# Two sequences feed the early expert tiles, routing goes out in steps, and the next tile's rows are turned between the two products

## The chip, the core and the metric

One Trainium2 chip, one of its cores. Its engines run side by side, each through its own queue of instructions in order: TensorE (PE, with its weight loads PEld), VectorE (DVE), ScalarE (ACT), GpSimd (POOL), and SyncE (SP), which issues most transfers. The metric is the device time of one launch in microseconds, lower is better.

## The reference

Block-sparse attention, then a cosine router that sends each token to one of eight experts. Shapes: 4 sequences, 8 heads, 768 tokens, head size 64; 3072 tokens of width 512; expert products 512x1024 and 1024x512, all in fp32.

```python
# q, k, v: (4, 8, 768, 64); the mask lets a block of 32 see its neighbours,
# the first and last block, and 3 sampled blocks
scores = where(mask, (q @ k.T) / sqrt(64), -1e9)
attn = softmax(scores) @ v
x = attn.transpose(0, 2, 1, 3).reshape(3072, 512)
xn = x / (norm(x) + 1e-6);  en = expert_emb / (norm(expert_emb) + 1e-6)
logits = xn @ en.T / tau                      # (3072, 8)
e = argmax(logits, 1)
gate = 1 / (sum(exp(logits - max(logits))) + 1e-9)
out[i] = gate[i] * (relu(x[i] @ w1[e[i]]) @ w2[e[i]])
```

## The kernel before

**Attention** (`attention_fast`) works on 16 pairs of heads, four pairs to a sequence. A pair has 12 units of work: two halves of the queries by six chunks of 128 keys. In a unit `u` TensorE multiplies scores for unit `u + 2` (`score_fast`, tile `sc`; the mask goes in as a small bf16 product), ScalarE takes the exponential (tile `e`), and TensorE multiplies `e` with `v` (`attend_fast`, tile `av`), while VectorE adds up the exponentials (tile `esum`). Every sixth unit ends a half: ScalarE copies one half of `av` to the tile `part` (L321), VectorE adds the other (tile `at`, L323), and the pair to come is turned (`turn_fast`, tiles `kt` and `qt`). `av` has one buffer: the next half's first product waits for `at`. Three units later `settle` turns the result back to rows (tile `back`) and divides by the sum. It also squares the rows on GpSimd (tile `sq`, L365) and adds the squares on VectorE (tile `nsq`, L366), for the norm. The small turns of `turn_fast`, `settle`, `rank`, `count` and `fill_slots` share one two-bank PSUM buffer (`two_banks`).

**Routing.** At the fifth unit of the next sequence `route` is issued for the finished one in a single piece: the norm's square root on GpSimd (L416), logits, maximum, one-hot choice and gate on VectorE, one exponential on ScalarE (L440), then the rows with their gate are written to `x_dram` (and `x_early`). Ten units later `rank` numbers the tokens of each expert. Once `EARLY` = 3 sequences are routed, `dispatch_early` picks `NE` = 11 tiles of 128 tokens, each tile of one expert alone, in six pieces at six units of the last sequence: counts, experts (`expert_e`), places, lanes (tile `lanes`), slots (`slot_e`). Two units later `fetch` is issued for the tiles 0 and 1: two loads of 2 MB for `w1` and `w2`, and one gather of the 128 rows (tile `xg`).

**Expert tiles** (`expert_tiles`). In all 27 tiles run: 24 always (`NE + NU`), the others under nested conditions on the number used. Each iteration fetches tile `i + 2` and runs `expert_tile(i)`: four turns of the gathered rows (tile `xg_ps`), a copy on VectorE (tile `xgt`), the first product in 64 matmuls into `hp` (two PSUM banks, two buffers), ReLU of its first half on ScalarE (L661) and of its second on VectorE (L662, both into `h`), the second product in 16 matmuls (tile `yp`), the gate on VectorE (tile `y`), and an indirect write to the output. The last sequence's `settle` and `route` are issued ahead of the first tile; its `rank` and `dispatch_late`, which finds the other tiles, lie between the first tiles (`between`), and must be through before tile `NE` is fetched.

A planner orders each engine's instructions by priority (the order of the program) among those whose inputs it expects to be ready, and sets all waits. Work under a condition stays in its block.

## Time and profile before

| | |
|---|---|
| median of 3 runs | 829.29 us (828.89 to 829.34) |
| profiled execution, its own time | 829.78 us |
| span of its instructions | 828.1 us |
| mean granted TensorE clock | 0.977 |
| TensorE busy | 768.2 us, 93% of the span |
| VectorE busy | 332.3 us, 40% |
| ScalarE busy | 200.6 us, 24% |
| GpSimd busy | 103.2 us, 12% |
| DMA, mean | 202 GB/s |

Times in the profile are microseconds from the start of the span. A matmul that is busy is not one at its peak, since matmuls overlap; so the pace of a stage is read from the distance of two starts. In brackets behind an instruction stands how long its engine sat idle before it, and what ended that.

### The profile page before, as it was taken

To read this page: it belongs to the slowest core of one execution; us is meant where nothing else is said; L and a number is where in the kernel's file an instruction comes from. 1 tells how busy PE (TensorE), PEld (TensorE's weight loads), DVE (VectorE), ACT (ScalarE), POOL (GpSimd) and SP (SyncE) were. 2 spreads that over 40 slices of the span, in tenths; PEclk is the share of its full clock that TensorE was granted. 3 is DMA by queue.
4 is the path that set the end of the run, shared out by engine and by line. 5 is a ranking of instruction groups with operands and counts; after the bars stand their busy time and mean duration, and the time that the engine had idled before them with its cause. 6 is when DMAs were issued, how large, how long until landed. Compare 5 with 4: busy or idle time off the path is not lost.

```text
span 828.1 us, 22309 instructions
## 1 busy us (share of the span) xinstructions
PE 768.2 (93%) x10026; PEld 502.6 (61%) x10026; DVE 332.3 (40%) x669; ACT 200.6 (24%) x292; POOL 103.2 (12%) x138
## 2 busy tenths in 40 slices
PE   5999979999799979789899999999999999999883
PEld 2555545555455545555667667677676776776661
DVE  3666666667666666755562111111111111111000
ACT  2555544554455534334100000000000000000000
POOL 2000010000100010030212011011010110100110
PEclk9999989999999999999899999999999999999997
DMA  4111243121411143750799889989888899888880
GB/s 155 31 51 58 60 152 119 61 59 61 182 47 51 54 172 99 272 188 4 281 331 313 293 309 323 315 308 326 318 307 308 303 331 319 297 317 304 287 288 16
DMA packets 64242, 167.04 MB, mean 202 GB/s; under 512 B 3004, under 2 KB 15292, under 8 KB 63238
## 3 DMA queue, kind: packets, MB, share of 16 engines
q1 hardware_dynamic: 59382, 151.17, 52.9%
q0 software_dynamic: 4480, 13.91, 4.3%
q8 instruction: 82, 1.34, 0.6%
q10 hardware_dynamic: 272, 0.39, 0.1%
q14 instruction: 26, 0.21, 0.1%
HBM read 148.14 MB, written 18.11 MB: 201 GB/s over the span
## 4 chain that ended last, share of the span: by engine, by line
PE 80%; DVE 6%; issue 6%; ACT 3%; DMA 1%; POOL 1%; SPq 0%; POOLq 0%; ACTq 0%
PE hp L658 21%; PE yp L666 20%; PE sc L296 17%; PE av L317 15%; PE turn L279 2%; PE back L352 2%; ACT h L661 2%; DVE esum L314 2%; PE back L345 1%; ACT e L299 1%; DMA out_dram<-y,slot_l 1%; POOL nrm L416 1%; DMA emb<-in_moe_expert_emb_dram 1%; DVE nsq L366 0%; DVE x L360 0%
## 5 line engine op out<-in xcount | busy, mean ns | idle before, releaser
L658 PEld LDWEIGHTS hp<-xgt,w 128*128 128x128 f32 x1728 | 200.5, 193 | 30.2 <-ACT h L661 12.4
L658 PE MATMUL hp<-xgt,w 128*128 128x128 f32 x1728 | 206.7, 278 | 12.7 <-ACT h L661 6.9
L666 PE MATMUL yp<-w,h 128*128 128x512 f32 x432 | 189.9, 592 | 0.0
L299 ACT ACTIVATE e<-sc 128x768 f32<-128x768 f32 x192 | 155.5, 810 | 132.9 <-PE sc L296 132.8
L317 PE MATMUL av<-e,vld 64*64 64x384 f32 x1536 | 169.3, 504 | 15.7 <-DVE at L323 15.1
L296 PE MATMUL sc<-qt,kt 64*64 64x384 f32 x1536 | 165.2, 495 | 0.0
L314 DVE TENSOR_TENSOR esum<-esum,e 128x768 f32<-128x768 f32 x128 | 122.4, 956 | 71.8 <-ACT e L299 69.6
L666 PEld LDWEIGHTS yp<-w,h 128*128 128x128 f32 x432 | 80.0, 190 | 90.4 <-issue 90.2
L661 ACT ACTIVATE h<-hp 128x512 f32<-128x512 f32 x27 | 16.1, 597 | 381.0 <-PE hp L658 381.0
L317 PEld LDWEIGHTS av<-e,vld 64*64 64x64 f32 x1536 | 53.0, 135 | 67.6 <-issue 23.7
L296 PEld LDWEIGHTS sc<-qt,kt 64*64 64x64 f32 x1536 | 62.0, 137 | 40.7 <-issue 38.0
L668 DVE TENSOR_SCALAR y<-yp,xg 128x512 f32<-128x512 f32 x27 | 20.3, 751 | 158.4 <-PE yp L666 158.4
L296 PE MATMUL sc<-qmask,kmask 64*64 64x384 bf16 x768 | 69.8, 333 | 0.0
L365 POOL TENSOR_TENSOR sq<-x 128x384 f32<-128x384 f32 x32 | 26.5, 827 | 332.3 <-DVE part L367 237.2
L662 DVE TENSOR_SCALAR h<-hp 128x512 f32<-128x512 f32 x27 | 18.7, 692 | 110.2 <-PE hp L658 110.2
L296 PEld LDWEIGHTS <-kmask 64*64 64x64 bf16 x768 | 26.0, 110 | 33.3 <-issue 32.5
L651 DVE COPY xgt<-xg_ps 128x512 f32<-128x512 f32 x27 | 18.6, 691 | 64.1 <-PE xg_ps L649 64.1
L669 POOL DMA_INDIRECT out_dram<-y,slot_l x16 | 16.4, 1026 | 208.2 <-DVE y L668 193.9
L312 DVE TENSOR_TENSOR esum<-e 128x768 f32<-128x768 f32 x32 | 30.7, 958 | 14.7 <-ACT e L299 14.7
L352 PE MATMUL back<-ones,esum 64*64 64x1 f32 x1536 | 28.5, 192 | 2.3 <-issue 2.2
L669 POOL DMA_INDIRECT out_dram<-y,slot_e x11 | 12.7, 1159 | 136.9 <-DVE y L668 124.3
L352 PEld LDWEIGHTS back<-ones,esum 64*64 64x64 f32 x1536 | 27.1, 137 | 2.8 <-issue 2.8
(153 smaller groups left out, 376.6 us busy)
## 6 DMA issues: line engine op xcount, KB each, us to landing
w<-in_moe_w_dram SPq DMA_DIRECT2D x58, 2048.0 KB, 10.4
x_dram<-x SPq DMA_DIRECT2D x4, 1539.0 KB, 10.4
kld<-in_k_dram SPq DMA_DIRECT2D x16, 384.0 KB, 4.4
vld<-in_v_dram SPq DMA_DIRECT2D x16, 384.0 KB, 3.3
qld<-in_q_dram SPq DMA_DIRECT2D x15, 384.0 KB, 4.8
x_early<-x SPq DMA_DIRECT2D x3, 1539.0 KB, 5.4
qld<-in_q_dram ACTq DMA_DIRECT2D x1, 384.0 KB, 3.4
xg<-x_dram,slot_l POOLq DMA_INDIRECT x18, 7.4
```

The lines of the kernel that those rows point to most:

```text
L296: nc.tensor.matmul(ps[D * r:D * (r + 1), h, 0:HALF], lhsT=rows[D * h:D * (h + 1), keys], rhs=cols[D * h:D * (h + 1), queries], start=first ...
L299: nc.scalar.activation(e, ps[:, :, 0:HALF], ACT.Exp)
L312: nc.vector.tensor_tensor(out=k.esum, in0=k.first, in1=e, op=ALU.add)
L314: nc.vector.tensor_tensor(out=k.esum, in0=k.esum, in1=e, op=ALU.add)
L317: nc.tensor.matmul(k.av[D * h:D * (h + 1), r, 0:HALF], lhsT=v[D * r:D * (r + 1), h, kc, :], rhs=e[D * r:D * (r + 1), h, :], start=(kc == 0 ...
L352: nc.tensor.matmul(sums[D * s:D * (s + 1), t, h, r:r + 1], lhsT=esum[D * r:D * (r + 1), h, cols], rhs=k.ones[D * r:D * (r + 1), 0:1], star ...
L365: nc.gpsimd.tensor_tensor(out=sq, in0=x, in1=x, op=ALU.mult)
L658: nc.tensor.matmul(hp[:, f, :], lhsT=w1[:, d, f * P:(f + 1) * P], rhs=xt[:, d, :], start=(d == 0), stop=(d == ND - 1))
L661: nc.scalar.activation(h[:, 0:half], hp[:, 0:half], ACT.Relu)
L666: nc.tensor.matmul(yp, lhsT=h[:, f, :], rhs=w2[:, f, :], start=(f == 0), stop=(f == NF - 1))
L668: nc.vector.tensor_scalar(out=y, in0=yp, scalar1=x[:, DM:XW], scalar2=None, op0=ALU.mult)
L669: nc.gpsimd.indirect_dma_start(out=k.out[:, :], out_offset=bass.IndirectOffsetOnAxis(ap=slot, axis=0), in_=y[:, :], in_offset=None, bounds ...
```

## The change

`EARLY` goes from 3 to 2, so that `NE` is 5 and not 11, `NG` 26 and not 20, `NU` 19 and not 13; the number of tiles that always run stays 24. In `settle` the squares on GpSimd and their sums on VectorE go; `route` takes the norm with six `Square` activations of 128x512 on ScalarE instead, each with its sum. `route` becomes a generator of ten steps, `rank` and `dispatch_early` follow as steps (seven of the latter, the lanes in two), and each unit of attention runs one step (`after_sequence`). After the second sequence the steps go on with `fetch` of the tiles 0 and 1 and, 12 units later, with `prepare(0)`, which turns the rows of tile 0 while attention still runs. In `expert_tile` the first product has two PSUM tiles, one for each half, and `prepare(i + 1)` stands between the two products. The last sequence's `settle` and `route` move in between the halves of tile 0's first product. The pool `sp` has three buffers for two.

```diff
...
 DM, E, F = H * D, 8, 1024
 ND, NF = DM // P, F // P
 G = 128
-EARLY = B - 1
+EARLY = 2
 NE = (EARLY * S - E * (G - 1) + G - 1) // G
 NG = (N + E * (G - 1)) // G - NE
 NU = N // G - NE
...
     b, j = g // NPAIR, g % NPAIR
     if w % (2 * NPAIR) == 0:
         k.x[b] = k.xp.tile([P, NC, XW], F32, name="x", tag="x")
-        k.nsq[b] = k.xp.tile([P, NPAIR, NC], F32, name="nsq", tag="nsq")
         k.part[b] = k.xp.tile([P, NC, H, E], F32, name="part", tag="part")
     ps = two_banks(k, "back")
     W = D + E
...
     nc.vector.tensor_tensor(
         out=k.x[b][:, chunks, j * P:(j + 1) * P].rearrange("p t (h d) -> p t h d", h=2),
         in0=rows[:, :, :, 0:D], in1=inv.unsqueeze(3).broadcast_to([P, NQ, 2, D]), op=ALU.mult)
-    x = k.x[b][:, chunks, j * P:(j + 1) * P]
-    sq = k.sp.tile([P, NQ, P], F32, name="sq", tag="sq")
-    nc.gpsimd.tensor_tensor(out=sq, in0=x, in1=x, op=ALU.mult)
-    nc.vector.reduce_sum(out=k.nsq[b][:, j, chunks], in_=sq, axis=AX.X)
     nc.vector.tensor_tensor(out=k.part[b][:, chunks, 2 * j:2 * j + 2, :], in0=rows[:, :, :, D:W],
                             in1=inv.unsqueeze(3).broadcast_to([P, NQ, 2, E]), op=ALU.mult)
 
...
 
     nc, p, x = k.nc, k.rp, k.x[b]
     nrm = p.tile([P, NC], F32, name="nrm")
-    if k.exact:
-        for c in range(NC):
-            sq = p.tile([P, DM], F32, name="sq")
-            nc.scalar.activation(sq, x[:, c, 0:DM], ACT.Square, accum_out=nrm[:, c:c + 1])
-    else:
-        nc.vector.reduce_sum(out=nrm, in_=k.nsq[b].rearrange("p j c -> p c j"), axis=AX.X)
+    for c in range(NC):
+        sq = p.tile([P, DM], F32, name="sq")
+        nc.scalar.activation(sq, x[:, c, 0:DM], ACT.Square, accum_out=nrm[:, c:c + 1])
+        yield
     nc.gpsimd.tensor_tensor(out=nrm, in0=nrm, in1=k.half, op=ALU.pow)
-    nc.vector.tensor_scalar(out=nrm, in0=nrm, scalar1=1e-6, scalar2=None, op0=ALU.add)
-    nc.vector.reciprocal(out=nrm, in_=nrm)
 
     def wide(t):
         return t.unsqueeze(2).broadcast_to([P, NC, E])
...
     lg = logits(k, x) if k.exact else l
     if not k.exact:
         nc.vector.reduce_sum(out=l, in_=k.part[b].rearrange("p c h e -> p c e h"), axis=AX.X)
+    yield
+    nc.vector.tensor_scalar(out=nrm, in0=nrm, scalar1=1e-6, scalar2=None, op0=ALU.add)
+    nc.vector.reciprocal(out=nrm, in_=nrm)
     m = p.tile([P, NC], F32, name="mx")
     nc.vector.tensor_tensor(out=l, in0=lg, in1=wide(nrm), op=ALU.mult)
     nc.vector.reduce_max(out=m, in_=l, axis=AX.X)
     nc.vector.tensor_tensor(out=l, in0=l, in1=wide(m), op=ALU.subtract)
-
+    yield
+    ex = p.tile([P, NC, E], F32, name="ex_l")
+    nc.scalar.activation(ex, l, ACT.Exp)
     oh = k.oh[:, b * NC:(b + 1) * NC, :]
     pick = p.tile([P, NC, E], F32, name="pick")
     nc.vector.tensor_scalar(out=pick, in0=l, scalar1=0.0, scalar2=None, op0=ALU.is_equal)
     nc.vector.tensor_tensor(out=pick, in0=pick, in1=k.rev.unsqueeze(1).broadcast_to([P, NC, E]), op=ALU.mult)
     nc.vector.reduce_max(out=m, in_=pick, axis=AX.X)
     nc.vector.tensor_tensor(out=oh, in0=pick, in1=wide(m), op=ALU.is_equal)
-
+    yield
     gate = p.tile([P, NC], F32, name="gate")
-    nc.scalar.activation(l, l, ACT.Exp)
-    nc.vector.reduce_sum(out=gate, in_=l, axis=AX.X)
+    nc.vector.reduce_sum(out=gate, in_=ex, axis=AX.X)
     nc.vector.tensor_scalar(out=gate, in0=gate, scalar1=1e-9, scalar2=None, op0=ALU.add)
     nc.vector.reciprocal(out=x[:, :, DM:XW], in_=gate.unsqueeze(2))
     for dram in (k.x_early, k.x_dram):
         if dram is k.x_dram or b < EARLY:
             nc.sync.dma_start(out=dram[b * S:(b + 1) * S, :].rearrange("(p c) w -> p (c w)", c=NC),
                               in_=x.rearrange("p c w -> p (c w)"))
+    for c in range(NC):
+        t = b * NC + c
+        nc.gpsimd.tensor_tensor(out=k.seen[:, t + 1, :], in0=k.seen[:, t, :], in1=k.oh[:, t, :], op=ALU.add)
+    yield
 
 
 def rank(k, b):
...
     nc, p = k.nc, k.rp
     oh = k.oh[:, b * NC:(b + 1) * NC, :]
     pick = p.tile([P, NC, E], F32, name="mine")
-    for c in range(NC):
-        t = b * NC + c
-        nc.gpsimd.tensor_tensor(out=k.seen[:, t + 1, :], in0=k.seen[:, t, :], in1=k.oh[:, t, :], op=ALU.add)
     rk = two_banks(k, "rk")[:, 0, 0:NC * E].rearrange("p (c e) -> p c e", e=E)
     nc.tensor.matmul(rk, lhsT=k.before, rhs=oh, start=True, stop=False)
     nc.tensor.matmul(rk, lhsT=k.ones, rhs=k.seen[:, b * NC:(b + 1) * NC, :], start=False, stop=True)
...
 
 def split_lanes(k, low, nt):
 
-    lanes = k.dp.tile([P, nt, P], BF16, name="lanes")
+    k.lanes = k.dp.tile([P, nt, P], BF16, name="lanes")
     for t in range(0, nt, NC):
-        k.nc.vector.tensor_tensor(out=lanes[:, t:t + NC], in0=k.lane.unsqueeze(1).broadcast_to([P, NC, P]),
+        k.nc.vector.tensor_tensor(out=k.lanes[:, t:t + NC], in0=k.lane.unsqueeze(1).broadcast_to([P, NC, P]),
                                   in1=low[:, t:t + NC].unsqueeze(2).broadcast_to([P, NC, P]), op=ALU.is_equal)
-    return lanes
+        yield
 
 
 def fill_slots(k, lanes, val, nt, tiles, name):
...
     k.fetched[i] = (w1, w2, x, slot)
 
 
-def expert_tile(k, i):
+def prepare(k, i):
+
+    x = k.fetched[i][2]
+    if i == 0:
+        ps = two_banks(k, "first")[:, 0].rearrange("p (d t) -> p d t", d=ND)
+    else:
+        ps = ring(k, "xg_ps", i, 1, k.eps, [P, ND, P])
+    for d in range(ND):
+        k.nc.tensor.transpose(ps[:, d, :], x[:, d * P:(d + 1) * P], k.ident)
+    k.turned_rows[i] = ring(k, "xgt", i, 2, k.wp, [P, ND, P])
+    k.nc.vector.tensor_copy(out=k.turned_rows[i], in_=ps)
+
+
+def expert_tile(k, i, meanwhile=None):
     nc = k.nc
     w1, w2, x, slot = k.fetched.pop(i)
-    ps = ring(k, "xg_ps", i, 1, k.eps, [P, ND, P])
-    for d in range(ND):
-        nc.tensor.transpose(ps[:, d, :], x[:, d * P:(d + 1) * P], k.ident)
-    xt = ring(k, "xgt", i, 2, k.wp2, [P, ND, P])
-    nc.vector.tensor_copy(out=xt, in_=ps)
-
-    hp = ring(k, "hp", i, 2, k.eps, [P, NF, P])
+    xt = k.turned_rows.pop(i)
     h = ring(k, "h", i, 2, k.wp2, [P, NF, P])
     half = NF // 2
-    for f in range(NF):
-        for d in range(ND):
-            nc.tensor.matmul(hp[:, f, :], lhsT=w1[:, d, f * P:(f + 1) * P], rhs=xt[:, d, :],
-                             start=(d == 0), stop=(d == ND - 1))
-        if f == half - 1:
-            nc.scalar.activation(h[:, 0:half], hp[:, 0:half], ACT.Relu)
-    nc.vector.tensor_scalar(out=h[:, half:NF], in0=hp[:, half:NF], scalar1=0.0, scalar2=None, op0=ALU.max)
-
+    for f0 in (0, half):
+        hp = ring(k, f"hp{f0}", i, 2, k.eps, [P, half, P])
+        for f in range(half):
+            for d in range(ND):
+                nc.tensor.matmul(hp[:, f, :], lhsT=w1[:, d, (f0 + f) * P:(f0 + f + 1) * P], rhs=xt[:, d, :],
+                                 start=(d == 0), stop=(d == ND - 1))
+        if f0 == 0:
+            nc.scalar.activation(h[:, 0:half], hp, ACT.Relu)
+            if meanwhile:
+                meanwhile()
+        else:
+            nc.vector.tensor_scalar(out=h[:, half:NF], in0=hp, scalar1=0.0, scalar2=None, op0=ALU.max)
+
+    if i + 1 < NE + NG:
+        prepare(k, i + 1)
     yp = ring(k, "yp", i, 1, k.eps, [P, DM])
     for f in range(NF):
         nc.tensor.matmul(yp, lhsT=h[:, f, :], rhs=w2[:, f, :], start=(f == 0), stop=(f == NF - 1))
...
         out=k.out[:, :], out_offset=bass.IndirectOffsetOnAxis(ap=slot, axis=0),
         in_=y[:, :], in_offset=None, bounds_check=N - 1, oob_is_err=False,
     )
+
+
+def after_sequence(n, b):
+
+    yield route(n, b)
+
+    def finish():
+        yield
+        yield
+        rank(n, b)
+        yield
+    yield finish()
+    if b == EARLY - 1:
+        yield dispatch_early(n)
+
+        def prefetch():
+            fetch(n, 0)
+            yield
+            fetch(n, 1)
+            for _ in range(12):
+                yield
+            prepare(n, 0)
+            yield
+        yield prefetch()
 
 
 def attention_fast(n, ctx):
...
         if u % NC == 3 and u > NC:
             settle(n, u // NC - 1)
         if u >= per * NPAIR and u % (per * NPAIR) == 4:
-            route(n, u // (per * NPAIR) - 1)
-        if u >= per * NPAIR and u % (per * NPAIR) == 14:
-            rank(n, u // (per * NPAIR) - 1)
-        if u in early:
-            next(steps)
-        if u == early[-1] + 2:
-            fetch(n, 0)
-            fetch(n, 1)
+            steps = chain(*after_sequence(n, u // (per * NPAIR) - 1))
+        next(steps, None)
         attend_fast(n, u)
         if u + 2 < units:
             score_fast(n, u + 2)
-def expert_tiles(n, between=()):
+def expert_tiles(n, between=(), first=None):
     between = iter(between)
     for i in range(NE + NU):
         if i + 2 == NE:
             for _ in between:
                 pass
         fetch(n, i + 2)
-        expert_tile(n, i)
+        expert_tile(n, i, first if i == 0 else None)
         next(between, None)
     used = n.nc.values_load(n.used[0:1, 0:1], min_val=0, max_val=NG)
     with ExitStack() as more:
...
 
         n.small = pool("small", 1, space=PSUM)
         n.dp, n.wp = pool("dp", 1), pool("wp", 1)
-        n.xp, n.rp, n.sp = pool("xp", 2), pool("rp", 2), pool("sp", 2)
+        n.xp, n.rp, n.sp = pool("xp", 2), pool("rp", 2), pool("sp", 3)
         with ExitStack() as attn:
             attention_fast(n, attn)
         n.wp2, n.eps = pool("wp2", 1), pool("eps", 1, space=PSUM)
 
         def between():
-            yield
             rank(n, B - 1)
-            yield
             late = dispatch_late(n)
             next(late)
             yield
...
             count_good(n)
             yield
 
-        settle(n, 2 * B * NPAIR - 1)
-        route(n, B - 1)
-        expert_tiles(n, between())
+        def last_rows():
+            settle(n, 2 * B * NPAIR - 1)
+            for _ in route(n, B - 1):
+                pass
+
+        expert_tiles(n, between(), last_rows)
 
 
 def exact(n):
```

## Rows read from the trace of the kernel before

**Rows 1.** The chain that ended last, shares of the span by engine.

```profile
PE 80%; DVE 6%; issue 6%; ACT 3%; DMA 1%; POOL 1%; SPq 0%; POOLq 0%; ACTq 0%
```

**Rows 2.** Timeline, ScalarE, L321: one row ends each half (start, duration).

```profile
28.53 0.47 ACT L321 COPY part<-av 128x384 f32<-128x384 f32 x1
...
103.65 0.47 ACT L321 COPY part<-av 128x384 f32<-128x384 f32 x1
118.88 0.47 ACT L321 COPY part<-av 128x384 f32<-128x384 f32 x1
...
143.00 0.47 ACT L321 COPY part<-av 128x384 f32<-128x384 f32 x1
...
327.50 0.47 ACT L321 COPY part<-av 128x384 f32<-128x384 f32 x1
...
375.05 0.47 ACT L321 COPY part<-av 128x384 f32<-128x384 f32 x1
...
396.05 0.48 ACT L321 COPY part<-av 128x384 f32<-128x384 f32 x1 [0.99 <-PE av L317]
```

**Rows 3.** Timeline around the first route.

```profile
114.52 1.36 POOL L416 TENSOR_TENSOR nrm<-nrm,half 128x6 f32<-128x6 f32 x1 [0.89 <-DVE nrm L415]
...
119.99 1.56 PE L317 MATMUL av<-e,vld 64*64 64x384 f32 x8 [4.24 <-DVE at L323]
...
121.65 1.50 PE L296 MATMUL sc<-qt,kt 64*64 64x384 f32 x8
```

**Rows 4.** Timeline during the early dispatch and the first fetches.

```profile
331.18 0.36 PE L468 MATMUL cp<-seen,ones 128*128 128x8 f32 x2 [1.65 <-ACT qt L283]
...
339.16 1.82 DVE L531 TENSOR_TENSOR lanes<-lane,low 128x768 bf16<-128x768 f32 x2
...
346.64 1.46 PE L317 MATMUL av<-e,vld 64*64 64x384 f32 x8 [1.85 <-DVE at L323]
...
366.37 0.31 PE L352 MATMUL back<-ones,esum 64*64 64x1 f32 x7 [0.44 <-issue]
```

**Rows 5.** Groups by line: mean ns of one, idle before, and what ended it.

```profile
L299 ACT ACTIVATE e<-sc 128x768 f32<-128x768 f32 x192 | 155.5, 810 | 132.9 <-PE sc L296 132.8
...
L366 DVE TENSOR_REDUCE nsq<-sq 128x3 f32<-128x384 f32 x32 | 17.7, 554 | 24.5 <-POOL sq L365 24.5
...
L165 ACT ACT_TABLE_LOAD x1 | 1.3, 1283 | 1.3 <-PEq L870 1.3
...
L165 ACT ACTIVATE emb_sq<-emb 8x512 f32<-8x512 f32 x1 | 0.6, 628 | 5.2 <-DMA emb<-in_moe_expert_emb_dram 5.2
```

**Rows 6.** Timeline: a tile in the steady stage, TensorE.

```profile
614.44 3.73 PE L658 MATMUL hp<-xgt,w 128*128 128x128 f32 x32
...
618.01 0.60 PE L649 MATMUL xg_ps<-ident,xg 128*128 128x128 f32 x4
...
618.86 3.84 PE L658 MATMUL hp<-xgt,w 128*128 128x128 f32 x32 [0.25 <-ACT h L661]
...
622.54 7.03 PE L666 MATMUL yp<-w,h 128*128 128x512 f32 x16
...
629.41 3.73 PE L658 MATMUL hp<-xgt,w 128*128 128x128 f32 x32
```

**Rows 7.** Timeline: tile 1's first product, then a conditional tile and the last gate.

```profile
418.07 3.73 PE L658 MATMUL hp<-xgt,w 128*128 128x128 f32 x32
...
765.77 3.84 PE L658 MATMUL hp<-xgt,w 128*128 128x128 f32 x32 [1.08 <-DVE xgt L651]
770.34 3.84 PE L658 MATMUL hp<-xgt,w 128*128 128x128 f32 x32 [0.74 <-ACT h L661]
...
814.53 0.75 DVE L668 TENSOR_SCALAR y<-yp,xg 128x512 f32<-128x512 f32 x1 [6.11 <-PE yp L666]
```

**Rows 8.** Busy time by stretch: PE, PEld, DVE, ACT, POOL, PEclk, DMA share, GB/s.

```profile
105.00:133.00 28.00, 23.76 (x488) 12.96 (x488) 17.76 (x40) 11.26 (x18) 4.93 (x9) 0.88 0.43 157
...
469.00:750.00 281.00, 276.28 (x1568) 199.31 (x1569) 40.48 (x57) 10.91 (x19) 37.17 (x36) 1.00 0.90 313
```

More of the change, by code (lines that the diff above doesn't have):

```diff
@@ L1 @@
 from contextlib import ExitStack
+from itertools import chain
 import dataclasses
@@ L72, in build_consts @@
     k.lane = iota(k, "lane", [P, P], [[1, P]])
-    k.by_g = iota(k, "by_g", [P, N // G + 1], [[G, N // G + 1]])
+    k.by_g = iota(k, "by_g", [P, NG + 1], [[G, NG + 1]])
     k.tile_no = iota(k, "tile_no", [P, NG], [[1, NG]])
@@ L579, in dispatch_early @@
     yield
-    lanes = split_lanes(k, low, nt)
-    yield
-    k.slots = [fill_slots(k, lanes, val, nt, NE, "slot_e")]
+    yield from split_lanes(k, low, nt)
+    k.slots = [fill_slots(k, k.lanes, val, nt, NE, "slot_e")]
     yield
@@ L609, in dispatch_late @@
     low, val = split_places(k, pos, NT, NG)
-    lanes = split_lanes(k, low, NT)
+    for _ in split_lanes(k, low, NT):
+        pass
     yield
-    k.slots.append(fill_slots(k, lanes, val, NT, NG, "slot_l"))
+    k.slots.append(fill_slots(k, k.lanes, val, NT, NG, "slot_l"))
     yield
@@ L699, in attention_fast @@
     score_fast(n, 1)
-    steps = dispatch_early(n)
-    early = [EARLY * per * NPAIR + i for i in (18, 20, 22, 24, 26, 31)]
+    steps = iter(())
     for u in range(units):
@@ L750, in attention_exact @@
             if (u - 1) % (H * NC) == 0:
-                route(n, (u - 1) // (H * NC) - 1)
+                for _ in route(n, (u - 1) // (H * NC) - 1):
+                    pass
                 rank(n, (u - 1) // (H * NC) - 1)
-def expert_tiles(n, between=()):
+def expert_tiles(n, between=(), first=None):
     between = iter(between)
@@ L786, in between @@
         def between():
-            yield
             rank(n, B - 1)
-            yield
             late = dispatch_late(n)
@@ L795, in between @@
             yield
-        settle(n, 2 * B * NPAIR - 1)
-        route(n, B - 1)
-        expert_tiles(n, between())
+        def last_rows():
+            settle(n, 2 * B * NPAIR - 1)
+            for _ in route(n, B - 1):
+                pass
+        expert_tiles(n, between(), last_rows)
 def exact(n):
@@ L819, in exact @@
         fetch(n, 1)
+        prepare(n, 0)
         expert_tiles(n)
@@ L843 @@
     n.loaded, n.vs, n.es, n.ets, n.sums, n.x, n.fetched = {}, {}, {}, {}, {}, {}, {}
-    n.turned, n.done, n.part, n.nsq = {}, {}, {}, {}
+    n.turned, n.done, n.part, n.turned_rows = {}, {}, {}, {}
     n.exact = False
```

## The prediction, made before the result was known

> **What bounds the kernel now.** I read the chain first: TensorE carries 80% of it, so only what makes TensorE wait, or gives it less to do, can move the time [rows 1]. The next view is the timeline of one instruction that closes every half of a pair, ScalarE's copy of `av`; the reader is to see its pace. Eight undisturbed ends stand 75.12 apart, 10.73 for a half. From first to last there are 31 halves in 367.52, and 31 x 10.73 = 332.7, so 34.9 us of attention are disturbance. The three halves from 103.65, with the first `route` and `rank`, hold 39.35 - 32.19 = 7.2 of it; the three from 327.50, with the early dispatch and the first fetches, 47.55 - 32.19 = 15.4; the other two sequences' `route` and `rank` the remaining 12.3 [rows 2]. What such a stall is, the timeline around `route` shows: VectorE waits in its queue for GpSimd's square root, 1.36 us, `at` lies behind it, and TensorE stands for 4.24 us. Behind the stop it runs on its lower clock of 1.2 GHz for a while: the granted clock of the 28 us around the `route` is 0.88 in the mean, and eight score products take 1.50, where a whole unit has 10.73 / 6 = 1.79 [rows 3, 8]. In the dispatch the stops are of several kinds: 1.65 for the shared PSUM buffer, 1.85 for `at` behind the lanes (1.82 for two pieces), and gaps of 0.44 between small matmuls in which nothing shown is waited for, five of them in one `settle` [rows 4].
>
> The second stage is the expert tiles. In a steady one TensorE's starts say where 14.97 us go (614.44 to 629.41): 3.57 half a first product, 0.85 turns of the next rows and a wait for the ReLU of that half, 3.68 the other half, 6.87 the second product [rows 6]. In a conditional block nothing can be moved in between, and two waits stand open, 1.08 for the copy of the rows and 0.74 for the ReLU [rows 7]. DMA is busy to 0.90 meanwhile [rows 8].
>
> **The change, part by part.** Sums are made against the profiled execution's 829.78 us, 0.49 above the median of the runs.
>
> *Routing in steps.* The long queue on VectorE is cut: at most five small operations or one lanes piece a unit, and the square root gets a unit of its own before its reader. What comes in its place is on ScalarE: six `Square`s in six consecutive units. None of this shape is in the trace; an 8x512 one took 0.63, and a 128x768 exponential 0.81 [rows 5]. I take 0.81, since the sum must be read out too, and keep 0.63 as the lower bound. A half has six exponentials and two half-size evacuations of about 0.47 [rows 2], 6 x 0.81 + 0.94 = 5.8 us; with six `Square`s 10.7 us, which is just the 10.73 that the half lasts. So ScalarE is full for one half, and TensorE, which waits for each exponential, is held now and then: I take 1.1 us a sequence (0 with the price of 0.63; 3 if each of six exponentials is 0.5 late). The backlog on VectorE falls on the unit in which `at` is due: 1.0 (0 to 2). `rank` still stops TensorE at the shared buffer: 0.5. In all 2.6 x 3 = 7.8 where 7.2 + 12.3 = 19.5 were: 11.7 gained. What VectorE no longer does, 32 sums of 0.55 and 24.5 us of waiting for GpSimd [rows 5], I count at nothing: `esum` and `at` are on time in an undisturbed half anyway, with TensorE's own work as their cover. The third buffer of `sp` I count at nothing too, for the same reason; if `esum` or `at` should come late after all, it gives some of the stalls back.
>
> Here a rule speaks against the change. The row first: one table load is in the whole trace, 1.28 us at L165, a `Square`, and 192 exponentials follow without another [rows 5]; so I price a switch between the two at nothing. The Trainium skill (ScalarE: Activation LUTs, section "Table sets: the hidden batching unit") says that activation functions are loaded as sets and that a function of another set costs a load each time. By the row the sum stays as it is; by the rule, were the two in different sets, it would grow by the amount worked out as the third rival below.
>
> *Early dispatch, fetch, first turn.* Instead of six pieces two units apart it has seven in consecutive units, over 12 chunks rather than 18. VectorE's work is a third smaller, but still more than the free part of each unit, so some of it ends up ahead of `at`: 3 us (0 to 6). The fetches go from the last sequence to the third; their 8 MB and POOL's gathers still run beside attention, and the unexplained gaps of the issue may come along: 2.5 (0 to 5, the length of the five gaps with the half clock behind them). On SP the loads of later pairs queue behind them, but those are needed a pair later. `prepare(0)` adds four turns and perhaps a wait for the shared buffer: 0.8 (0.4 to 2). Together 6.3 where 15.4 were: 9.1 gained.
>
> *The seam.* Attention's last product ends at about 396.05 [rows 2], and tile 1's first product starts at 418.07 [rows 7]: 22.0 us for one tile and a `settle`. With rows turned and weights landed before, tile 0's first half needs only its PSUM bank, which the last scores have left; `at` and the late `settle` hide behind that half. Then: 3.57 + 3.68 + 0.45 for turns + 6.87 = 14.6, `settle`'s 72 small matmuls 1.3 (seven took 0.31 [rows 4], so 3.2 at most), and 1.0 for a ReLU that sits behind `route` on VectorE (0 to 2.6). 16.8 us: 5.2 gained (2 to 7). There is no idle stretch for the clock to fall in.
>
> *The tile.* With a tile for each half nothing that the second half writes is still being read, so I take the wait as gone, and the turns cost only themselves: four at the pace of the products (3.57 / 32 = 0.11) are 0.45. They go between the products, where the ReLU of the second half (0.7 on VectorE, needed half-way through the second product, some 3.4 us later) and the copy of the rows (needed a product later) are covered. 3.57 + 3.68 + 0.45 + 6.87 = 14.57, 0.40 less than now. From tile 1's first product to the last gate there are 396.5 us now (418.07 to 814.53 [rows 7]). After: 26 x 14.57 = 378.8; plus 2.0 for `rank`, `count` and slots, which now lie in waits and then don't; plus 0.7 for one turn of rows that no tile uses and a late first gather. 381.5: 15.0 gained, 1.7 to 2.2 of it in each conditional block. Bounds: 4 if the wait stays in another place, 18 if the two allowances vanish. The late dispatch must now be through before tile 5 is fetched and not tile 11; SP waits for its experts, the weights behind it, but with three buffers of weights TensorE feels that only some 30 us later.
>
> The sum: 11.7 + 9.1 + 5.2 + 15.0 = 41.0; 829.78 - 41.0 - 0.5 = **788 us**.
>
> **The rivals.** *First: tiles keep their pace.* The wait before the second half may belong to something else than the shared tile, or DMA may be the true limit. For it: DMA is already busy to 0.90 at 313 GB/s. Against: 313 x 14.97 / 14.57 = 322 GB/s would make 0.93 of it, TensorE waits for no weights now, and in every steady tile the row that ends the wait is that ReLU [rows 6, 8]. Then 26 x 14.97 + 2.7 = 391.9, 4.6 gained instead of 15.0: 799 us.
>
> *Second: attention keeps half of its stalls.* ScalarE is at its limit in three halves, or the dispatch steps, now one a unit, pile up. For it: 10.7 of 10.73 us. Against: no step waits for a chain on another engine as `route` did. At half of the 20.8: 799 us.
>
> *Third, the other side: `Square` and the exponential displace each other's tables.* Each of 18 `Square`s in attention would bring two loads of 1.28 us. ScalarE would need 0.81 + 0.81 + 2.57 = 4.2 us for a unit, 2.4 over the mean 1.79, 43 us in all, and some 6 more at half clock: 838 us. It decides from 41 / 18 = 2.3 us a `Square`. Against it stands the single load of the trace [rows 5]. The skill's page gives a switch as about 2.66 us with its drain; by that estimate the loss would be about twice as large.
>
> *Fourth:* first and second together, 810 us.
>
> **How the numbers follow.** Forecast 0.62 (778 to 797), first rival 0.13, second 0.13, fourth 0.03, third 0.02; 0.05 for more gain than forecast, where the gaps of the issue and ScalarE's load cost nothing (under 778); 0.02 for no change. From the terms' bounds alone the ends would be 774 and 813. The range 776 to 804 takes in the first two rivals and leaves out the fourth, the third and the edge of the better case. A measurement of this kernel tells 0.2% (1.7 us) from no change. Faster holds all but the third rival and the last case: 0.96; same 0.02; slower 0.02.
>
> **What would show it.** Ends of halves 10.7 apart but for 2 to 3 us more around each `route`, and no half clock there; `e` waiting for `Square` on ScalarE in six units a sequence; one table load; tile starts 14.5 to 14.6 apart, with no wait of the second half for a ReLU, in the conditional blocks too; tile 1 starting 16 to 18 us after the last `part`. Wrong would be: steady tiles at 15.0; waits of `hp` on weights; a gap in front of tile 5; halves of 13 us or more at the routes or around the early fetch; several table loads.

## The result, and the profile after

The changed kernel takes 809.12 us (806.98 to 811.44, 4 runs) against 829.32 for the one before (828.89 to 830.02): 0.9756 of the time [0.9719, 0.9793] (in square brackets behind a ratio stands its 95% interval). It is faster, but by 20 us where 41 were forecast, and 809 lies outside the range of 776 to 804. The profiled execution took 811.13.

Each term can be read from the same rows as before. First the copies of `av` that end the halves (timeline, ScalarE), against [rows 2]:

```profile
28.56 0.47 ACT L322 COPY part<-av 128x384 f32<-128x384 f32 x1
...
92.94 0.47 ACT L322 COPY part<-av 128x384 f32<-128x384 f32 x1
105.62 0.48 ACT L322 COPY part<-av 128x384 f32<-128x384 f32 x1 [0.30 <-PE av L318]
120.88 0.47 ACT L322 COPY part<-av 128x384 f32<-128x384 f32 x1
132.97 0.47 ACT L322 COPY part<-av 128x384 f32<-128x384 f32 x1
145.25 0.47 ACT L322 COPY part<-av 128x384 f32<-128x384 f32 x1
...
398.18 0.48 ACT L322 COPY part<-av 128x384 f32<-128x384 f32 x1 [0.99 <-PE av L318]
```

Attention lasts 398.18 - 28.56 = 369.6, 2.1 longer than before, where 20.8 were to be saved. An undisturbed half is 10.73 as it was. The four halves from 92.94 hold 12.68, 15.26, 12.09 and 12.28: 9.4 over, where the prediction had 2.6 for a sequence. What happens in them is in the timeline of the same stretch:

```profile
100.62 0.82 PE L297 MATMUL sc<-qt,kt 64*64 64x384 f32 x8
...
101.98 0.63 ACT L408 ACTIVATE sq<-x 128x512 f32<-128x512 f32 x1 [2.13 <-DVE x L360]
...
102.52 0.19 ACT L408 ACTIVATION_READ_ACCUMULATOR sq<-x 128x1 f32 x1
102.61 0.61 ACT L408 ACTIVATE sq<-x 128x512 f32<-128x512 f32 x1
...
103.22 0.61 ACT L408 ACTIVATE sq<-x 128x512 f32<-128x512 f32 x1
...
103.83 1.49 ACT L300 ACTIVATE e<-sc 128x768 f32<-128x768 f32 x2
...
104.67 0.88 PE L318 MATMUL av<-e,vld 64*64 64x384 f32 x8 [1.78 <-ACT e L300]
...
114.72 0.63 ACT L408 ACTIVATE sq<-x 128x512 f32<-128x512 f32 x1 [2.13 <-DVE x L360]
...
118.14 0.17 DVE L420 TENSOR_SCALAR nrm<-nrm 128x6 f32<-128x6 f32 x1 [2.45 <-POOL nrm L410]
...
120.04 0.24 ACT L428 ACTIVATE ex_l<-l 128x48 f32<-128x48 f32 x1 [2.68 <-DVE l L425]
...
120.74 0.21 DVE L434 TENSOR_TENSOR oh<-pick,mx 128x48 f32<-128x48 f32 x1
...
120.88 0.47 ACT L322 COPY part<-av 128x384 f32<-128x384 f32 x1
...
121.38 0.56 DVE L324 TENSOR_TENSOR at<-av,part 128x384 f32<-128x384 f32 x1 [0.33 <-ACT part L322]
121.99 1.56 PE L318 MATMUL av<-e,vld 64*64 64x384 f32 x8 [2.20 <-DVE at L324]
```

The reader is to see that nothing stands one step a unit. Three `Square`s run in a row from 101.98, the moment `settle` has written the rows (`x`, L360), and three more from 114.72. The scores of the next exponential were through at 101.44, yet it starts at 103.83, behind the third `Square`; TensorE stops for 1.78 each time. The Trainium skill (Perfetto Trace Analysis, section "Tensor Engine Instruction (MATMUL, LD_WEIGHTS)") says in passing that ScalarE and VectorE work their queues strictly first in, first out; these rows agree. Then VectorE runs the chain from `nrm` to `oh` nearly in one go, 118.14 to 120.95 with one `esum` in between, and `at` comes behind it. The row of `at` names one wait more, 0.33 for `part`: ScalarE has the routing's own exponential (`ex_l`) ahead of the next exponential and of `part`, and stood for 2.68 until the chain had its `l`. So the chain holds `at` up in two queues at once. TensorE stops for 2.20, after which eight products take 1.56 on the lower clock (0.51 granted from 121.90 to 123.60).

The seam, TensorE and ScalarE (timeline), against [rows 7]:

```profile
394.55 0.63 ACT L408 ACTIVATE sq<-x 128x512 f32<-128x512 f32 x1 [2.13 <-DVE x L360]
...
397.24 0.88 PE L318 MATMUL av<-e,vld 64*64 64x384 f32 x8 [2.53 <-ACT e L300]
...
399.31 6.65 PE L664 MATMUL hp<-xgt,w 128*128 128x128 f32 x32 [1.19 <-DVE at L324]
...
418.42 1.35 PE L664 MATMUL hp<-xgt,w 128*128 128x128 f32 x10
```

From the last half's end to tile 1's first product it is 20.2 us, with 16.8 forecast and 22.0 before. Here too three hoisted `Square`s hold up the last exponential, and behind that stop the first 32 products take 6.65 at the lower clock (0.56 granted from 399.20 to 406.00).

Tiles on TensorE, a steady one, then a conditional one and the last gate (timeline), against [rows 6, 7]:

```profile
622.25 7.31 PE L664 MATMUL hp<-xgt,w 128*128 128x128 f32 x64
629.40 0.60 PE L649 MATMUL xg_ps<-ident,xg 128*128 128x128 f32 x4
629.84 7.03 PE L677 MATMUL yp<-w,h 128*128 128x512 f32 x16
...
781.20 7.31 PE L664 MATMUL hp<-xgt,w 128*128 128x128 f32 x64
...
795.86 0.75 DVE L679 TENSOR_SCALAR y<-yp,xg 128x512 f32<-128x512 f32 x1 [6.02 <-PE yp L677]
```

No wait is left in a tile, in the conditional blocks neither. Starts stand 14.45 apart; tile 1's first product to the last gate takes 795.86 - 418.42 = 377.4, which is 19.0 less than before (15.0 forecast). The sum, -2.1 + 1.8 + 19.0 = 18.7, is the difference of the two profiled executions, 18.65. In the windows of [rows 8] TensorE's clock around the route is 0.94 and its products are busy through all 281 us of the tiles, with DMA at 0.90 as before:

```profile
105.00:133.00 28.00, 24.02 (x496) 13.06 (x492) 17.11 (x38) 13.54 (x25) 3.33 (x7) 0.94 0.43 157
469.00:750.00 281.00, 281.00 (x1626) 205.83 (x1625) 40.03 (x59) 11.35 (x19) 37.79 (x37) 1.00 0.90 326
```

So the question is why the steps brought nothing, and whether they would, if they stood where the program puts them.

### The profile page after: what moved, and what is told of

It is laid out like the page before. It is cut to its first block, busy times and chain, and to the rows that moved or that the text cites. A ratio compares the mean times of both kernels' runs of the same rounds, so it can differ in the third digit from the quotient of the medians.

```text
span 809.4 us, 22268 instructions
## 1 busy us (share of the span) xinstructions
PE 759.3 (94%) x10024; PEld 495.4 (61%) x10024; DVE 315.8 (39%) x633; ACT 215.0 (27%) x340; POOL 74.4 (9%) x106
## 4 chain that ended last, share of the span: by engine, by line
PE 80%; DVE 6%; issue 5%; ACT 4%; DMA 1%; POOL 1%; SPq 0%; POOLq 0%; ACTq 0%
PE hp L664 21%; PE yp L677 20%; PE sc L297 17%; PE av L318 15%; PE turn L280 3%; ACT e L300 2%; PE back L352 2%; ACT sq L408 2%; DVE esum L315 2%; PE xg_ps L649 1%; PE back L345 1%; DMA out_dram<-y,slot_l 1%; DVE x L360 1%; DMA emb<-in_moe_expert_emb_dram 1%; POOL nrm L410 1%
## 5 line engine op out<-in xcount | busy, mean ns | idle before, releaser
L664 PE MATMUL hp<-xgt,w 128*128 128x128 f32 x1728 | 201.1, 278 | 1.2 <-DVE at L324 1.2
L318 PE MATMUL av<-e,vld 64*64 64x384 f32 x1536 | 167.1, 496 | 22.6 <-ACT e L300 14.6
L297 PE MATMUL sc<-qt,kt 64*64 64x384 f32 x1536 | 163.4, 489 | 0.0
L318 PEld LDWEIGHTS av<-e,vld 64*64 64x64 f32 x1536 | 50.5, 134 | 80.3 <-ACT e L300 43.6
L671 DVE TENSOR_SCALAR h<-hp 128x512 f32<-128x512 f32 x27 | 18.7, 691 | 159.8 <-PE hp L664 159.6
L680 POOL DMA_INDIRECT out_dram<-y,slot_l x22 | 22.3, 1014 | 267.5 <-DVE y L679 255.5
L410 POOL TENSOR_TENSOR nrm<-nrm,half 128x6 f32<-128x6 f32 x4 | 5.4, 1342 | 340.8 <-ACT sq L408 340.8
L284 ACT ACTIVATE qt<-turn 128x384 f32<-128x384 f32 x32 | 15.7, 490 | 52.7 <-DVE kt L283 52.7
L324 DVE TENSOR_TENSOR at<-av,part 128x384 f32<-128x384 f32 x32 | 17.8, 557 | 23.6 <-ACT part L322 23.6
L352 PE MATMUL back<-ones,esum 64*64 64x1 f32 x1536 | 26.4, 190 | 0.0
## 6 DMA issues: line engine op xcount, KB each, us to landing
w<-in_moe_w_dram SPq DMA_DIRECT2D x58, 2048.0 KB, 10.1
```

The costliest lines, as they stand in the source:

```text
L297: nc.tensor.matmul(ps[D * r:D * (r + 1), h, 0:HALF], lhsT=rows[D * h:D * (h + 1), keys], rhs=cols[D * h:D * (h + 1), queries], start=first ...
L318: nc.tensor.matmul(k.av[D * h:D * (h + 1), r, 0:HALF], lhsT=v[D * r:D * (r + 1), h, kc, :], rhs=e[D * r:D * (r + 1), h, :], start=(kc == 0 ...
L352: nc.tensor.matmul(sums[D * s:D * (s + 1), t, h, r:r + 1], lhsT=esum[D * r:D * (r + 1), h, cols], rhs=k.ones[D * r:D * (r + 1), 0:1], star ...
L664: nc.tensor.matmul(hp[:, f, :], lhsT=w1[:, d, (f0 + f) * P:(f0 + f + 1) * P], rhs=xt[:, d, :], start=(d == 0), stop=(d == ND - 1))
L671: nc.vector.tensor_scalar(out=h[:, half:NF], in0=hp, scalar1=0.0, scalar2=None, op0=ALU.max)
L680: nc.gpsimd.indirect_dma_start(out=k.out[:, :], out_offset=bass.IndirectOffsetOnAxis(ap=slot, axis=0), in_=y[:, :], in_offset=None, bounds ...
```

## The experiments

The kernels were run in three groups, each on another chip; the kernel before, run beside each, took 824.33, 829.68 and 824.84 us. So kernels of different groups are compared by their ratio to it.

**Does the cut into steps do anything?** The changed kernel with all of `route` issued in one unit:

```diff
-    yield route(n, b)
+    for _ in route(n, b):
+        pass
+    yield iter((None,) * 10)
```

> The changed kernel with all of `route` issued in one unit again; the later steps keep their units. Theory: the planner gives the steps no force, since it runs an instruction as soon as its inputs are ready, so nothing changes: within 2 us of the changed kernel's 809 us, the ends of halves around the first `route` again 12.7, 15.3 and 12.1 apart. Rival: the steps work, and it is only the work on ScalarE that costs; then one piece brings back the stop of 4.2 us at each of three routes: 815 us or more.

807.00 us, 0.978 [0.976, 0.980]: the interval overlaps with that of the changed kernel's 0.9756. TensorE's products around the first route (timeline) have the same waits, to the hundredth:

```profile
117.33 0.88 PE L318 MATMUL av<-e,vld 64*64 64x384 f32 x8 [1.78 <-ACT e L300]
121.91 1.56 PE L318 MATMUL av<-e,vld 64*64 64x384 f32 x8 [2.20 <-DVE at L324]
```

The steps of `route` have no force. They set an order of the program, and in this trace the planner gives an instruction its place by when its inputs are ready.

**The tile part alone.** The kernel before with `prepare` and `expert_tile` of after, routing and dispatch untouched:

```diff
         settle(n, 2 * B * NPAIR - 1)
         route(n, B - 1)
+        prepare(n, 0)
```

> The kernel before with only the expert tile changed: a PSUM tile for each half and the next rows turned between the products. Theory: all of the change's gain comes from here, 19 us between tile 1's first product and the last gate, tile starts 14.45 apart: 810 us, as much as the whole change. Rival: part of it comes from the earlier fetches and the smaller early dispatch: 815 to 820 us.

806.55 us, 0.9784 [0.9767, 0.9801]. From tile 5's start to the last gate it takes 318.10, the changed kernel 318.11. The changed kernel with `route` in one piece took 807.00 beside it: the gain of the whole change is that of its tile part, and the other edits together bring nothing that shows.

**The steps held in their units.** A helper keeps what a step issues behind the last instruction already issued on the engines named; first on ScalarE and VectorE:

```diff
+def held(n, go):
+    last = {}
+    for i in reversed(n.nc.cur_bb.bb.instructions):
+        last.setdefault(i.engine, i)
+    with ExitStack() as stay:
+        for e in (mybir.EngineType.Activation, mybir.EngineType.DVE):
+            stay.enter_context(n.tc.issue_after(last[e]))
+        go()
...
-        next(steps, None)
+        held(n, lambda: next(steps, None))
...
-                meanwhile()
+                held(k, meanwhile)
```

> The changed kernel with each step's instructions on ScalarE and VectorE queued behind what the program has issued there before, so that the planner can't move them ahead; also the last `route` behind tile 0's ReLU. Theory (it is the place that costs): single `Square`s cost 0.2 to 0.3 each, the chain no longer stops TensorE and the clock stays up; 12 to 18 us gained, 791 to 797 us. Rival (ScalarE is too full wherever they stand): each `Square` keeps its price of 0.65, only the chain's 2.4 and the clock's 1.5 go at two or three places: 800 to 806 us.

785.69 us, 0.9531 [0.9515, 0.9547]: the forecast's 788 of 829.8 would be 0.950. That is faster than the theory's 791 to 797 and the rival's 800 to 806: the order costs more than I had priced it at. Run again in the third group:

> The steps held on both engines, again, beside held_act and the kernel with the squares on GpSimd. Theory: some 39 to 42 us faster than before, ratio 0.949 to 0.953, as the prediction's sum had it. Rival (the prediction's sizes were met by luck of one chip): ratio over 0.957.

786.02 us, 0.9530 [0.9514, 0.9545].

**Which engine's order matters?** The same with only ScalarE, or only VectorE, in the loop over engines.

> Steps kept in their unit on ScalarE alone; VectorE's part of the routing may still be moved. Theory (the order is at fault on two engines, and each has its own price): the Squares go one a unit and give back most of what their block cost, some 2 x 1.9 us a sequence and 1.6 in the last one, 11 to 13 us; the chain on VectorE still runs in one go ahead of `at`, so its 2.4 and the half clock stay. Some 30 us faster than before, ratio 0.961 to 0.967, and halves with a route of about 10.73 + 0.6 for the Squares, then 12 to 13 for the chain. Rival (the two are one matter: the chain starts when the last Square lands, and once the Squares are spread it starts late enough to lie in a free place): as fast as with both engines held, ratio 0.953. Other rival (ScalarE was never the matter): no faster than the change as it is, 0.976.

> Steps kept in their unit on VectorE alone; the six Squares may still be moved. Theory (two prices): `at` is not late behind the chain any more, 3 x 2.4 us and the half clock behind it come back, 8 to 11 us; the Squares still stand three in a row ahead of an exponential, with a stop of TensorE of about 1.8 us at each block. Some 28 us faster than before, ratio 0.964 to 0.970; halves of about 12.7 where the Squares are, 11 to 12 where the chain is. Rival (the Squares' block alone stops TensorE, the chain only fills the stop): ratio 0.975, as the change.

ScalarE alone: 787.51 us, 0.9490 [0.9476, 0.9505]. VectorE alone: 802.99 us, 0.9666 [0.9645, 0.9688]. For ScalarE alone the theory of two separate prices fell: it brings all of the gain. VectorE alone came in where its theory had it, so VectorE's order has a price too, as long as ScalarE's is free. To compare it with both engines held, in one group:

> The steps held on ScalarE alone, beside the kernel with both engines held on one chip. Theory (once the Squares stand a unit apart, it matters little whether the chain on VectorE is cut): the same within 3 us, slower by 0.6 a sequence, some 2 us, for a chain that runs in one go; ratio 0.949 to 0.954. Rival (holding VectorE costs something elsewhere, as between the two chips it seemed): faster by 3 us or more than with both held.

785.50 us, 0.9524 [0.9508, 0.9541], beside 0.9530 with both held: the same. Its ends of halves and the stretch of the first route, on ScalarE, then TensorE (timeline), and the window:

```profile
27.59 0.47 ACT L322 COPY part<-av 128x384 f32<-128x384 f32 x1
...
102.70 0.47 ACT L322 COPY part<-av 128x384 f32<-128x384 f32 x1
...
112.04 0.62 ACT L408 ACTIVATE sq<-x 128x512 f32<-128x512 f32 x1
...
112.72 0.81 ACT L300 ACTIVATE e<-sc 128x768 f32<-128x768 f32 x1
113.43 0.62 ACT L408 ACTIVATE sq<-x 128x512 f32<-128x512 f32 x1
...
114.04 0.47 ACT L322 COPY part<-av 128x384 f32<-128x384 f32 x1
...
125.01 0.47 ACT L322 COPY part<-av 128x384 f32<-128x384 f32 x1
...
128.99 0.23 ACT L428 ACTIVATE ex_l<-l 128x48 f32<-128x48 f32 x1
...
138.18 0.47 ACT L322 COPY part<-av 128x384 f32<-128x384 f32 x1
...
375.41 0.48 ACT L322 COPY part<-av 128x384 f32<-128x384 f32 x1 [0.99 <-PE av L318]
```

```profile
118.57 0.88 PE L318 MATMUL av<-e,vld 64*64 64x384 f32 x8 [0.28 <-ACT e L300]
...
127.29 0.88 PE L318 MATMUL av<-e,vld 64*64 64x384 f32 x8 [0.91 <-DVE at L324]
```

```profile
105.00:133.00 28.00, 26.45 (x604) 15.26 (x600) 19.02 (x42) 17.49 (x33) 4.15 (x7) 1.00 0.33 108
```

A `Square` now stands between two exponentials, and the stop behind it is 0.28 in place of 1.78, with one more of 0.35 for `at`. The last `Square` comes a unit's step later than the one before, so the chain on VectorE starts later too; it still runs nearly in one go, but costs one stop of 0.91, and the clock stays at 1.00. The routing's exponential now stands at 128.99, behind `part`, and ScalarE no longer waits for the chain. That is the second thing that the order on ScalarE mends; no run with the `Square`s on ScalarE mends one of the two alone. The three halves from 102.70 last 35.48, 3.3 over 32.19 (2.6 forecast). Attention lasts 347.8, the seam 17.4.

**The squares back on GpSimd.** `settle` squares on GpSimd and sums on VectorE as before, `route` in steps, first without and then with `held` on both engines. `k.exact` marks a second path of the program, which is not the one in these traces; the pool `sp` goes back to two buffers as well:

```diff
+    sq = k.sp.tile([P, NQ, P], F32, name="sq", tag="sq")
+    nc.gpsimd.tensor_tensor(out=sq, in0=x, in1=x, op=ALU.mult)
+    nc.vector.reduce_sum(out=k.nsq[b][:, j, chunks], in_=sq, axis=AX.X)
...
-        sq = p.tile([P, DM], F32, name="sq")
-        nc.scalar.activation(sq, x[:, c, 0:DM], ACT.Square, accum_out=nrm[:, c:c + 1])
+        if k.exact:
+            sq = p.tile([P, DM], F32, name="sq")
+            nc.scalar.activation(sq, x[:, c, 0:DM], ACT.Square, accum_out=nrm[:, c:c + 1])
...
+    if not k.exact:
+        nc.vector.reduce_sum(out=nrm, in_=k.nsq[b].rearrange("p j c -> p c j"), axis=AX.X)
...
-        n.xp, n.rp, n.sp = pool("xp", 2), pool("rp", 2), pool("sp", 3)
+        n.xp, n.rp, n.sp = pool("xp", 2), pool("rp", 2), pool("sp", 2)
```

> The changed kernel with the norm's squares on GpSimd and their sums on VectorE in `settle`, as in the kernel before; the rest of the change stays. Theory: three `Square`s in a row hold an exponential back and cost TensorE 1.95 us at each of seven places, so some 12 to 14 us are gained: 795 to 798 us, halves without `route`'s VectorE chain at 10.7 again. Rival: the stalls are the VectorE chain's alone, and the squares only fill time in which ScalarE waits anyway: 806 us or more.

800.84 us, 0.9716 [0.9699, 0.9733]: 6 us better than the change with `route` in one piece beside it, half of what I expected. Without the `Square`s the chain comes sooner, and the stop moves to it. On VectorE and TensorE (timeline):

```profile
115.79 0.17 DVE L428 TENSOR_SCALAR nrm<-nrm 128x6 f32<-128x6 f32 x1 [1.47 <-POOL nrm L418]
...
118.52 0.55 DVE L324 TENSOR_TENSOR at<-av,part 128x384 f32<-128x384 f32 x1
...
119.13 1.56 PE L318 MATMUL av<-e,vld 64*64 64x384 f32 x8 [3.49 <-DVE at L324]
```

VectorE waits for the square root with `at` queued behind the chain, as in [rows 3], and TensorE's stop grows from 2.20 to 3.49. From the ends of the halves the three routes cost 21.4 here, 28.0 in the changed kernel.

> The squares of the norm on GpSimd and their sums on VectorE as in the kernel before, every step kept in its unit on both engines. It prices six Squares on ScalarE where each stands in its own unit. Theory (a Square a unit costs TensorE what the prediction took, 1.1 us a sequence, and the 32 sums on VectorE cost nothing): 1 to 4 us faster than the kernel with both engines held, ratio 0.949 to 0.953. Rival (VectorE's sums with their wait for GpSimd hold up `at` now that VectorE is on the path): slower than it, ratio over 0.956.

787.28 us, 0.9485 [0.9470, 0.9500], against 0.9716 without `held`. The three routes cost 5.6 in place of 21.4. So with no `Square` in attention at all the planner's order still costs some 2 per cent: most of the loss needs no row of `Square`s, the routing's chain alone makes it. Beside the others in one group:

> The squares on GpSimd, all steps held, beside the same kernel with the Squares on ScalarE. Its halves with a route lose 1.7 where the other's lose 2.7. Theory: 1 to 4 us faster than with the Squares on ScalarE. Rival (the sums on VectorE eat that up): the same within 1 us, or slower.

785.07 us, 0.9519 [0.9503, 0.9535], where both held with `Square`s took 786.02: the medians are 0.95 apart. The intervals of the ratios overlap, but each of its five runs (784.67 to 785.67) lies below each of the other five (785.88 to 786.68). So six `Square`s a sequence, each in its unit, cost about a microsecond in all over squares on GpSimd, their sums on VectorE and the smaller pool `sp`. In the halves they show as 114.04 - 102.70 = 11.34 and 125.01 - 114.04 = 10.97 (the rows of ScalarE alone, above), 0.85 a sequence over undisturbed ones; not all of that reaches the end.

**The two edits of the tile, one at a time**, from the kernel before: only a PSUM tile for each half (first), only the turns between the products (second).

```diff
-    hp = ring(k, "hp", i, 2, k.eps, [P, NF, P])
...
+    for f0 in (0, half):
+        hp = ring(k, f"hp{f0}", i, 2, k.eps, [P, half, P])
```

> The kernel before with one edit: a PSUM tile for each half of the first product; rows turned where they were. Theory (the tile's gain hangs on the shared PSUM tile, the turn of the rows was already moved between the halves by the planner): steady tiles 14.45 to 14.6 apart in place of 14.97; the three conditional ones keep their wait of 1.08 for the copy and lose the 0.74 behind the ReLU, 15.8 to 16.0 in place of 16.72; in all 11 to 14 us faster than before, ratio 0.983 to 0.987. Rival (the turn between the products is what pays): steady tiles at 14.9 to 15, ratio 0.995 to 1.

842.75 us, 1.0148 [1.0126, 1.0170]: slower than before, which neither the theory nor the rival had. Steady tiles stand 15.72 apart (TensorE, timeline):

```profile
610.17 7.41 PE L659 MATMUL hp<-xgt,w 128*128 128x128 f32 x64 [1.00 <-DVE xgt L651]
...
624.29 0.60 PE L649 MATMUL xg_ps<-ident,xg 128*128 128x128 f32 x4
625.89 7.41 PE L659 MATMUL hp<-xgt,w 128*128 128x128 f32 x64 [1.01 <-DVE xgt L651]
```

With the wait in the middle gone, the planner no longer puts the turns there. They stay at the tile's head, and the copy of the rows is waited for in every tile. Then the other half of the edit:

```diff
+    if i + 1 < NE + NG:
+        prepare(k, i + 1)
     yp = ring(k, "yp", i, 1, k.eps, [P, DM])
```

> The kernel before with the other half of the tile's change: the next rows turned between the two products, one PSUM tile for both halves of the first product. Theory (two waits, and each edit takes one: the second half behind the first half's ReLU, the first half behind the copy of its rows): the wait behind the ReLU stands open in every tile, since no turns lie there any more: 0.9 to 1.0 over the 14.45 of both edits together, 15.35 to 15.45 a tile, and as the two edits together were 17.8 faster than before, 26 x 0.95 less makes this one some 7 us slower than before, ratio 1.005 to 1.010. Rival (the planner puts the turns back into that wait): 14.97 a tile, 4 us faster than before, ratio 0.995.

818.39 us, 0.9927 [0.9909, 0.9945]; the rival held. The planner lifts the turns from between the products back into the wait for the ReLU, 14.97 a tile as before (TensorE, timeline):

```profile
625.79 0.60 PE L652 MATMUL xg_ps<-ident,xg 128*128 128x128 f32 x4
626.64 3.84 PE L666 MATMUL hp<-xgt,w 128*128 128x128 f32 x32 [0.25 <-ACT h L669]
```

Its conditional tiles fall from 16.72 to 15.01, since the turns now belong to the same block. So one edit alone loses 13 us, the other gains 6, and both gain 18.

## Why the prediction was wrong

*Routing in steps*: this step failed. It read "at most five small operations or one lanes piece a unit" and "six `Square`s in six consecutive units" off the program, and the planner does not keep to it. A yield between two instructions is no dependence. I had the counterexample in [rows 6], where the turns of the next rows stand in the middle of a tile and not at the head of one, and did not apply it to the routing. The term was 7.8; the three routes cost 28.0 and the last sequence's first three `Square`s another 1.6, from the ends of the halves. That is 29.6 in place of 19.5 before: a loss of 10.1, not a gain of 11.7. The price of six `Square`s in units of their own, 1.1 a sequence, was about right (0.85); the price of three in a row is the whole length of the row, 1.85, since an exponential whose scores are there stands behind it.

One reading behind this step was short as well. The stop of 4.24 in [rows 3] was put down to VectorE alone. The rows beside it, from the kernel before, name ScalarE too (timeline):

```profile
118.04 0.24 ACT L440 ACTIVATE l<-l 128x48 f32<-128x48 f32 x1 [4.95 <-DVE pick L434]
...
118.88 0.47 ACT L321 COPY part<-av 128x384 f32<-128x384 f32 x1
...
119.38 0.56 DVE L323 TENSOR_TENSOR at<-av,part 128x384 f32<-128x384 f32 x1 [0.34 <-ACT part L321]
```

ScalarE stood for 4.95 with the routing's exponential next in its queue and `part` behind it, and `part` was the last thing that `at` waited for; VectorE's chain had ended 0.3 earlier. The prediction counted on cutting VectorE's queue, and held against the second rival that no step waits for a chain on another engine. `ex_l` in the changed kernel is such a step, with a wait of 2.68.

That the order was at fault, and not the amount of work, is shown by `held`: with the order of the program enforced on ScalarE, attention lasts 347.8 (346.7 by the forecast), the seam 17.4 (16.8), the tiles 377.5 (381.5). With both engines held the three routes cost 8.4 (7.8). The forecast's 0.950 stands between 0.949 and 0.953; that it is met so closely is in part luck, since the 4.0 that the tiles bring beyond the forecast make up for what the other terms fall short of.

*Early dispatch, fetch, first turn*: 6.3 forecast; the four halves of 13.31, 14.15, 10.73 and 12.06 hold 7.3 over undisturbed ones. The size was right, but it is no fixed one: with `route` in one piece these halves hold 5.2, with both engines held 6.8 and 8.2 in its two runs.

*The seam*: 16.8 forecast, 20.2 measured. Tile 0 does start without waiting for weights or rows, but not ahead of `at`, as forecast: its first product waits 1.19 for it, in the changed kernel and with ScalarE held. The rest is the same fault, the exponential behind three `Square`s and the lower clock after that, of which I had written that there is no idle stretch for it. Held, it is 17.4.

*The tile*: the mechanism was right, the size small: 14.45 and not 14.57, since the second half now follows the first at 3.57 and not at the 3.68 I had kept from a half that starts after a wait; 26 x 0.12 = 3.1. Of the allowances of 2.7 there was 1.7 (377.4 - 26 x 14.45). The single-edit kernels show that there were two waits, 1.0 for the copy of the rows and 0.85 behind the ReLU, and that the planner already filled the second with the turns, so the gain needs both edits at once.

*The rivals*: the first fell, with tiles at 14.45 and 326 GB/s. The second had the right place: ScalarE in the routes' halves; but attention kept all its stalls, and ScalarE was not full: it waited. The third fell: one table load and 24 `Square`s (groups by line, after).

```profile
L166 ACT ACT_TABLE_LOAD x1 | 1.3, 1283 | 1.3 <-PEq L901 1.3
...
L408 ACT ACTIVATE sq<-x 128x512 f32<-128x512 f32 x24 | 14.8, 618 | 16.8 <-DVE x L360 16.8
```

So the Trainium skill's rule (ScalarE: Activation LUTs, section "Table sets: the hidden batching unit") did not bite: `Square` and the exponential need no switch here. 809 us is close to the fourth rival's 810, by other parts: nothing from attention and more from the tiles.

*The sums*: three do not come out as written. The seam's terms add up to 16.9, the fourth rival to 809, and the bounds of the four terms to 771 and 818 in place of 774 and 813.

What stays open: why the planner, which moves work by what it expects, puts a `Square` ahead of an exponential that TensorE waits for (its costs were not varied); and what makes the kernel before 5 us quicker in two of the groups than in the others. Where these 5 us lie can be read, since the kernels with a single edit of the tile have its attention unchanged. They lie in the half that ends at 375.05 [rows 2], the one with five gaps of 0.42 to 0.44 (one is in [rows 4]) in which nothing shown is waited for. In the kernel before it lasts 17.37, at a mean granted clock of 0.90. In the kernel with the turns between the products, of a quick group, it lasts 12.01 (356.51 to 368.52), without these gaps and at 1.00; the half behind it is 0.8 longer. In the one with a PSUM tile for each half, of the group of 829.68, it lasts 18.06, with five such gaps again. So part of the 15.4 us that the early dispatch cost, and with it of the 9.1 that were to be gained there, is not there in every group.

## What to carry to other kernels

Where a planner orders the queues, splitting work in the program is a wish, not an order: before a gain is counted for it, find in the trace whether the planner keeps to the program, and if not, tie the pieces to an instruction of the engine whose queue matters. Here it was enough to tie ScalarE, whose exponentials TensorE waits for: what a side chain puts into that queue, a row of `Square`s or one small exponential that is not ready, holds up everything behind it. And an edit that removes one wait can open another which the first had been covering: two such edits are to be judged together, 1.015 and 0.993 alone and 0.978 as a pair.

## What was not expected of the hardware

A `Square` of 128x512 takes 0.62 us, and the readout of its sum shows as 0.19 of its own. But the readout starts 0.09 before the `Square` ends (102.52), and the next `Square` starts at that end (102.61): in a row each takes 0.61 to 0.63 with its readout. And the lower clock is no fixed companion of the routing: behind the changed kernel's stops of 1.78 the products take 0.88 at a granted clock of 1.00, behind the one of 2.20 they take 1.56 at 0.51; with ScalarE held the stretch of the first route shows 1.00, where it was 0.94 in the changed kernel and 0.88 before [rows 8].
